# Attention and MLP on one core: masks ahead of the first scores, thirty copies on other engines, a fourth buffer, and another order of all items

## The chip, the cores and the metric

One core of a Trainium2 chip runs the whole program. The metric is the device time of one execution in microseconds. The kernel before takes 229.18 us (median of three runs, 229.06 to 229.55).

## What is computed

Inputs q, k, v have 4 batches x 8 heads x 768 positions x 64, in float32. Heads 0, 2 and 6 see all earlier positions (they are called retrieval heads here); the other five see the first 4 positions and a window of 64 (stream heads). The heads' outputs, side by side, are the 3072 x 512 input of an MLP with a learned slope for negative values:

```python
scores = q @ k.T / sqrt(64)                      # per batch and head
keep   = causal                  for heads 0, 2, 6
keep   = causal & (pos < 4 | rel < 64)   for the others
a = softmax(where(keep, scores, -1e9));  x = a @ v      # then (4*768, 512)
h = x @ w_in                                     # w_in 512 x 2048
g = maximum(h, 0) + alpha * minimum(h, 0)
out = g @ w_out                                  # w_out 2048 x 512
```

## The kernel before

**Segments.** Work on attention goes in 16 segments n, four to a batch; a segment is a pair of heads (line 99: (2,6), (1,5), (0,4), (3,7)), so segments 0, 4, 8, 12 hold two retrieval heads. The MLP goes in eight blocks t of 512 or 256 tokens, two to a batch.

**Items.** Every step is an item with a name, and a list of 1076 names, `ORDER` (line 14), says in which order they are emitted (line 806). An engine runs its own instructions in that order and nothing reorders them, so `ORDER` fixes the order on TensorE (PE), ScalarE (ACT), VectorE (DVE), GpSimd (POOL), and the order in which SyncE (SP) and POOL issue DMAs. The names, with n the segment, hh the head of the pair, m a part:

- `Lq`, `Lk`, `Lv`: loads of float32 rows into one of four buffers each of qf, kf, vf (lines 203 to 246), issued by SP. For n < 8, q rows are read as 1536-byte pieces and k as pieces of 1536 (retrieval) or 512 bytes (stream); v always, and q and k from n = 8, as rows of 256 bytes. `wi0` to `wi7` and `wo0` to `wo3` load the weights with a cast to bf16 on the way, issued by POOL (lines 690 to 697).
- `Cq`, `Ck`, `Cv`: casts to bf16; the strings at line 296 name the engine of each segment. `Tq`, `Tk` (n < 8): transposes on PE (line 355) of q and of both heads of k, and `tq`, `tk` copy them out of PSUM. From n = 8 a DMA transposes (`Dq`, `Dk`, on SP).
- `S`: scores on PE; `s`: exp on ACT. In segments 0 to 3 a mask is added on PE by a second matmul with the identity, right behind each score (lines 457 to 463); from segment 4 on DVE multiplies the exps by 0/1 masks (`m`, lines 473 and 526), which POOL builds (`nr`, `ns`, lines 658 and 662). Scores of segments from 4 on, of two heads, are gathered and emitted as a burst: each uses half of PE's rows, and the two halves run side by side (line 417); where one half has little work they run one after the other over all rows.
- `A`, `a`: product with v, and division by the sum; `X`: transposition into xT (by DMA, or on PE with a copy `x`).
- `P`, `p`, `g`: first MLP product on PE, max(-h, 0) on ACT into a buffer `neg`, and the slope on DVE (lines 588 to 611). `O`, `o`: second product and copy out on ACT, from where POOL (t < 6) or SP stores it. `L`, `l`: the last 128 rows in three column cuts. `warm`: matmuls on a zero tile.

**Order around the change.** PSUM has eight banks, given out at build time by `take` in the order of emission. The first MLP products (`P0`, `P1`: blocks 0 and 1) begin when the four segments of batch 0 are done, near 27 us, and fill PE until about 55 us; the transposes of segments 4 to 7 (`Tq5`, `Tk4`, `Tk5`, `Tk7`, `Tq4`, `Tk6`, `Tq6`) are strewn among them, and the scores of segment 4 follow. SP issues the loads for these segments in the order q5, k4, k5, k7, k6, q4, q6, v7, v5, q7, k8, v6, v4. A buffer is loaded again when its cast has been done.

Of the kernel before, what the change touches and what calls it, by code (L numbers as in the profile page):

```python
# [14 lines left out]
busy zero La id warm0 kz3 Lq0.0 sz1 vz2 nms nmr so1 vz0 Lq0.1 Lk1 warm8 warm5 warm3 kz1 qz0 one Lq1 Lk0 Ck0.0 Cq0.0  # L15
Tq0.0 tq0.0 Tk0.0 qz kz0 kz2 idf warm2 Lk2 tk0.0 Ck1.0 Ck1.1 Cq0.1 Tk1 S0.0.1 s0.0.1 Tq0.1 S0.0.0 Cq1 warm7 Lv0 tk1.0
sz2 vz1 vz3 Tq1 Lq2 Ck0.1 S0.0.2 s0.0.0 tk1.1 Tk0.1 Ck2.1 tq1 S1.1.0 s0.0.2 Ck2.0 warm4 tq0.1 nz0 s1.1.0 Cq2 tk0.1 Cv0
Lk3 S0.1.0 kfz0 Lv1 vo ro0 Ck3.1 s0.1.0 Lq3 Ck3.0 wi1 wi0 Cq3 sz0 S1.0.0 so2 Al s1.0.0 so0 al S0.1.1 s0.1.1 Lv2 Tq2
Tk2 tk2.1 tk2.0 S0.1.2 S1.0.1 A0.0 s0.1.2 a0.0 Cv1 A0.1 a0.1 Cv2 s1.0.1 tq2 S1.1.1 nz1 Tk3 S2.0.1 tk3.0 s1.1.1 S2.0.2
X0 s2.0.1 x0 wi6 s2.0.2 wi7 Lv3 Lq5 Tq3 tk3.1 S2.0.0 wi5 m4.0.2 warm6 S2.1.0 A1.0 a1.0 Lk4 s2.0.0 A2.0 S2.1.1 A1.1  # L20
a2.0 tq3 s2.1.0 a1.1 S3.0.0 s2.1.1 s3.0.0 A2.1 a2.1 S3.1.1 X1 S3.0.1 s3.0.1 Lk5 wi4 kfz2 Cv3.0 Cq5 Lk7 wi2 X2 Ck4.0
s3.1.1 S3.1.0 x1 P0.0.0 x2 P0.0.1 A3.0 P0.1.0 P0.1.1 Lk6 Lq4 Lq6 Ck4.1 kfz3 nr Cv3.1 s3.1.0 A3.1 Lv7 Lv5 Lq7 Ck5.0 wi3
a3.0 P0.2.0 Tq5 tq5 P0.3.0 P0.3.1 a3.1 X3 x3 ns kfz1 P0.2.1 Tk4 near2 P1.2 P0.1.2 P0.2.2 P0.0.2 p1.2 p0.1 g0.1 Ck5.1
P1.0 P0.3.2 g1.2 P0.15 tk4.0 p0.2 g0.2 p0.15 wo0 p1.0 Lk8 near0 g0.15 g1.0 ro1 P1.12 P1.14 m12.1.2 p0.0 g0.0 wo1 tk4.1
p1.12 P0.14 g1.12 p0.14 g0.14 P0.13 p0.13 g0.13 P0.11 p1.14 Tk5 Ck7.1 g1.14 P1.10 tk5.0 p0.11 p1.10 Ck6.0 Ck7.0 g0.11
m8.0.2 tk5.1 wo2 Lv6 Lv4 P0.10 P0.8 p0.8 Tk7 g1.10 wo3 Cq4 Lk9 P0.12 P1.8 p0.10 g0.8 p0.12 g0.10 Tq4 P0.6 P0.9 p0.3
Ck6.1 g0.3 tq4 P0.4.0 P0.5.0 Tk6 P0.4.1 p1.8 g1.8 tk7.0 p0.9 g0.9 Cq6 P0.5.1 P0.5.2 p0.5 g0.12 p0.6 tk6.1 P0.4.2 g0.6
g0.5 tk6.0 S4.0.5 P0.7 p0.7 P1.6 g0.7 P1.4 s4.0.5 p0.4 Tq6 m4.1.2 tk7.1 g0.4 Cv5 p1.6 g1.6 O0.1.0 tq6 S4.0.3 O0.2.0
O0.2.1 S5.1.1 S5.0.0 S4.0.1 S6.1.0 m14.0.2 p1.4 g1.4 s5.0.0 O0.1.1 s4.0.3 s4.0.1 O0.2.2 S5.0.2 S5.1.0 S4.0.2 S5.1.2
s6.1.0 m4.0.1 Cv7 O0.3.0 s5.0.2 s5.1.2 s5.1.1 s4.0.2 O0.1.2 s5.1.0 O0.1.3 o0.1 Cq7 Cv4 O0.3.1 m5.1.0 m8.1.2 m5.0.2  # L30
m4.0.3 m5.1.2 S4.0.0 S4.1.4 S5.0.1 S4.0.4 S4.1.0 s4.0.4 s5.0.1 Lk10 m5.0.1 O0.2.3 O0.3.2 Tq7 m5.0.0 o0.2 s4.1.0 m4.0.4
m5.1.1 A5.1 s4.0.0 m4.0.0 a5.1 O0.3.3 tq7 S7.0.0 S7.0.1 S4.1.3 S7.1.1 S6.0.5 S4.1.1 m4.0.5 s4.1.4 o0.3 Lq9 s4.1.3 Ck8
m4.1.3 A5.0 a5.0 X5 s4.1.1 A4.0 s7.0.0 s7.1.1 Lk11 Lq8 s7.0.1 a4.0 s6.0.5 near1 m7.0.0 m7.1.1 m4.1.0 O1.1.0 S7.1.0
S6.0.4 S7.0.2 S4.1.5 S6.0.1 S7.1.2 S6.1.1 O1.1.1 Cv6 s7.1.0 O1.0.0 s4.1.5 m7.0.1 s6.1.1 m4.1.5 m6.1.1 s7.1.2 m6.1.0
s7.0.2 m7.0.2 S6.0.2 S4.1.2 S6.1.2 S6.0.0 s6.0.4 s4.1.2 s6.0.1 s6.1.2 O1.0.1 m6.0.5 m7.1.0 m4.1.1 m4.1.4 m7.1.2 m6.1.2
S6.0.3 A4.1 s6.0.0 m6.0.0 m6.0.1 A7.1 O1.1.2 A6.1 s6.0.3 m6.0.4 m6.0.3 s6.0.2 a4.1 a6.1 A6.0 A7.0 a6.0 O1.1.3 O0.0.0
O0.0.1 O0.0.2 O1.0.2 m10.0.2 O1.0.3 O0.0.3 o0.0 X4 X6 a7.1 a7.0 X7 P2.9 P2.3 p2.9 P3.4 Ck9 Cq9 g2.9 P2.14 p2.14 g2.14
Cq8 p3.4 Lq10 Lq11 Dk8.0 P2.10 p2.10 Dk9.1 o1.0 p2.3 g2.3 g3.4 Dk8.1 P3.2 P3.14 P3.12 P2.8 Dq8 P2.1 P3.8 o1.1 p3.2
Dk9.0 Lv10 g2.10 Dq9 p3.14 P2.7 Ck10 g3.2 p3.12 g3.12 g3.14 P2.2 p2.2 g2.2 Cq10 Dq10 P2.11 p2.1 g2.1 p2.11 p2.8 g2.11
P3.6 P2.5 p2.5 g2.5 P2.13 p2.13 g2.8 g2.13 P2.0 p2.0 g2.0 p2.7 P3.0 p3.0 P2.4 S8.0.5 Lv8 Lv11 P2.15 P2.12 s8.0.5 Cq11  # L40
g3.0 p2.15 g2.7 g2.15 S8.0.0 p2.12 g2.12 Ck11 p3.6 S9.0.2 P2.6 p2.6 g3.6 s8.0.0 p2.4 g2.4 g2.6 s9.0.2 p3.8 P3.10 g3.8
p3.10 O3.0.0 O2.0.0 S8.1.5 s8.1.5 O3.0.1 O2.0.1 g3.10 m8.0.0 Cv8 S8.1.3 S9.0.0 S8.0.3 S9.1.1 S8.0.1 S9.1.0 s8.1.3
s9.1.0 s8.0.1 s9.0.0 s8.0.3 m8.0.3 m8.0.1 O2.0.2 O2.0.3 o2.0 Dk10.1 Lv9 m9.0.0 Cv9 m8.0.5 Dk11.0 m9.1.0 m9.0.2 S8.0.4
S9.0.1 S10.1.1 S8.1.4 Dq11 s8.1.4 Lq13 Lk13 O3.0.2 Dk10.0 s9.1.1 s10.1.1 s9.0.1 s8.0.4 O3.0.3 o3.0 Dk11.1 S10.1.0
S10.1.2 m9.0.1 S11.0.2 S9.1.2 S8.0.2 S11.0.0 s9.1.2 Cv10 m9.1.1 A9.0 s11.0.2 s10.1.0 O2.3.0 m9.1.2 A9.1 a9.0 a9.1 X9
s10.1.2 s11.0.0 O2.3.1 Lq15 Lv14 Lq12 S8.1.0 S11.0.1 S10.0.3 m10.1.0 s8.0.2 S10.0.1 S8.1.2 S8.1.1 S10.0.0 O2.3.2
s8.1.2 s8.1.0 m8.1.4 Cq13 s11.0.1 s8.1.1 m11.0.2 m10.1.2 m8.0.4 m11.0.0 A8.0 s10.0.0 m8.1.5 m10.1.1 O2.3.3 a8.0
S11.1.2 S10.0.4 S11.1.0 S10.0.5 S10.0.2 m8.1.3 m11.0.1 s10.0.3 s10.0.1 S11.1.1 s11.1.2 A10.1 s11.1.1 O2.2.0 O2.1.0
s10.0.4 m6.0.2 m10.0.1 Cv11 m8.1.1 m8.1.0 a10.1 m10.0.4 Ck13 m10.0.0 m11.1.2 A11.0 A8.1 O2.1.1 s10.0.2 s10.0.5 o2.3
s11.1.0 Dk13.0 m11.1.1 m10.0.3 m10.0.5 m11.1.0 A10.0 a11.0 a8.1 a10.0 O3.1.0 A11.1 Cq12 O2.2.1 O2.2.2 O2.2.3 a11.1 X8  # L50
# [796 lines left out]
```

## Time and profile before

| | |
|---|---|
| median of three runs | 229.18 us (229.06 to 229.55) |
| the profiled execution | 229.83 us, its span 228.0 us |
| matmuls on PE | 2005 |
| last matmul ends / span ends | 225.0 / 228.0 us |
| DMA over the span | 37.39 MB, mean 164 GB/s |

Busy time by stretch of the span, in us:

| stretch | PE | DVE | ACT | POOL | DMA share | GB/s |
|---|---|---|---|---|---|---|
| 0 to 30: batch 0's attention | 28.1 | 23.5 | 18.9 | 23.9 | 1.04 | 244 |
| 30 to 54: MLP blocks 0 and 1, first product | 24.0 | 18.1 | 21.4 | 8.2 | 1.19 | 222 |
| 54 to 78: batch 1's attention, second product | 23.3 | 18.0 | 18.5 | 3.6 | 0.97 | 207 |
| 78 to 103: blocks 2 and 3, first product | 25.0 | 16.9 | 13.2 | 1.6 | 0.99 | 192 |
| 103 to 126: batch 2's attention | 23.0 | 20.6 | 17.7 | 3.2 | 1.05 | 192 |
| 126 to 150: blocks 4 and 5, first product | 24.0 | 14.3 | 12.2 | 1.7 | 1.11 | 212 |
| 150 to 183: batch 3's attention | 33.0 | 22.5 | 19.9 | 3.1 | 0.51 | 102 |
| 183 to 205: blocks 6 and 7, first product | 22.0 | 13.7 | 12.0 | 0.5 | 0.06 | 25 |
| 205 to 228: their second product | 20.1 | 4.1 | 5.8 | 0.0 | 0.19 | 69 |

The DMA share is the mean busy share of the core's 16 DMA engines; it can pass 1 because transfers on one engine overlap. In the page and the views that follow, a row gives start and length of a group of instructions, the engine, the line, output <- inputs, and in brackets how long the engine stood idle before it and what ended that.

### The profile page before, as it was taken

How to read it: one execution, taken by the hardware profiler on the slowest of the kernel's cores; microseconds unless marked ns; L12 is line 12 of the kernel's file. 1: busy time of each engine (PE TensorE's matmuls, PEld its weight loads, DVE VectorE, ACT ScalarE, POOL GpSimd, SP SyncE). 2: the span in 40 equal slices, each digit the busy share in tenths (PEclk: the TensorE clock that was granted, in tenths of full speed). 3: DMA queues.
4: the chain of work that ended last, by engine and by line, in shares of the span. 5: the costliest groups of instructions: out<-in, count | busy, mean ns of one | idle time of the engine just before them, and what ended most of it. 6: DMA issues, size and time to landing. Idle time of an engine off the chain costs nothing.

```text
span 228.0 us, 5239 instructions
## 1 busy us (share of the span) xinstructions
PE 222.4 (98%) x2005; PEld 135.9 (60%) x2005; DVE 151.6 (66%) x395; ACT 139.6 (61%) x284; POOL 45.8 (20%) x91
## 2 busy tenths in 40 slices
PE   8999999999999999999999999999999999999994
PEld 8789876563455656555556455556556555664454
DVE  7769849966389816899699219987586535966000
ACT  2689559999799128477994136787594236563311
POOL 6769996101130001000400001000110110000000
PEclk9999999999999999999999999999999999999999
DMA  6999999999998798989969899995821420000213
GB/s 190 313 229 210 286 223 262 206 197 241 206 287 142 132 204 227 172 192 181 254 153 199 194 266 146 218 166 107 132 93 38 116 95 0 0 4 0 88 66 123
DMA packets 95417, 37.39 MB, mean 164 GB/s; under 512 B 82440, under 2 KB 93600, under 8 KB 95392
## 3 DMA queue, kind: packets, MB, share of 16 engines
q1 hardware_dynamic: 89136, 27.73, 61.2%
q0 software_dynamic: 5792, 8.93, 17.1%
q10 hardware_dynamic: 464, 0.40, 0.5%
q8 instruction: 15, 0.25, 0.5%
q14 instruction: 10, 0.08, 0.2%
HBM read 27.71 MB, written 6.29 MB: 149 GB/s over the span
## 4 chain that ended last, share of the span: by engine, by line
PE 92%; ACT 3%; DVE 2%; issue 1%; DVEq 0%; ACTq 0%
PE P L597 35%; PE P L617 34%; PE P L552 7%; PE P L430 4%; PE P L687 3%; PE P L413 2%; PE P L363 2%; PE P L636 2%; ACT neg L602 1%; PE P L501 1%; DVE kT L392 1%; PE P L423 1%; PE P L577 1%; ACT kT L392 1%; ACT eS L523 1%
## 5 line engine op out<-in xcount | busy, mean ns | idle before, releaser
L609 DVE SCALAR_TENSOR_TENSOR g<-neg,oma,P 128x256 bf16<-128x256 f32 (+1 forms) x128 | 71.0, 608 | 35.9 <-ACT neg L602 35.5
L597 PE MATMUL P<-xT,w_in_b 128*128 128x512 bf16 (+1 forms) x512 | 86.5, 326 | 0.0
L617 PE MATMUL P<-w_out_b,g 128*128 128x512 bf16 x368 | 85.4, 379 | 0.0
L602 ACT ACTIVATE neg<-P 128x512 f32<-128x512 f32 x96 | 54.4, 600 | 27.2 <-PE P L597 22.6
L597 PEld LDWEIGHTS <-w_in_b 128*128 128x128 bf16 x512 | 49.5, 98 | 31.7 <-DVE g L609 0.2
L617 PEld LDWEIGHTS <-g 128*128 128x128 bf16 x368 | 33.8, 98 | 37.2 <-issue 1.2
L469 ACT ACTIVATE eR<-P 128x448 bf16<-128x448 f32 (+4 forms) x63 | 37.1, 636 | 5.4 <-PE P L430 2.3
L623 ACT COPY ot<-P 128x512 f32<-128x512 f32 x23 | 13.8, 602 | 37.8 <-PE P L617 32.9
L627 POOL DMA_DIRECT2D out_dram<-ot x18 | 10.3, 571 | 113.2 <-ACT ot L623 113.0
L517 ACT ACTIVATE eS<-P 128x352 bf16<-128x352 f32 x45 | 21.0, 493 | 3.7 <-PE P L430 3.7
L563 DVE TENSOR_TENSOR xn<-P,rcp 128x448 bf16<-128x448 f32 (+1 forms) x32 | 19.5, 608 | 1.1
L528 DVE TENSOR_TENSOR eS<-eS,ms_near 128x352 bf16<-128x352 bf16 x45 | 14.3, 334 | 4.4 <-ACT eS L517 4.2
L479 DVE TENSOR_TENSOR eR<-eR,mr_near 128x128 bf16<-128x128 bf16 (+5 forms) x54 | 12.1, 252 | 4.0 <-ACT eR L469 4.0
L430 PE MATMUL P<-qT,kT 64*128 64x176 bf16 (+13 forms) x181 | 11.7, 251 | 0.3 <-DVE g L609 0.3
L430 PEld LDWEIGHTS <-kT 64*128 64x128 bf16 x181 | 7.2, 94 | 7.6 <-issue 6.8
L413 PE MATMUL P<-qT,kT 128*128 128x192 bf16 (+14 forms) x68 | 11.3, 251 | 0.3 <-ACT eS L523 0.3
L552 PE MATMUL P<-vb,eS 128*128 128x65 bf16 x260 | 11.0, 193 | 0.4 <-DVE eS L528 0.4
L552 PEld LDWEIGHTS <-eS 128*128 128x128 bf16 x260 | 9.7, 97 | 2.9 <-DVE eS L528 0.6
L562 DVE RECIPROCAL rcp<-P 128x7 f32<-128x7 f32 (+1 forms) x32 | 6.3, 198 | 7.1 <-PE P L552 6.9
L552 PE MATMUL P<-vb,eR 128*128 128x65 bf16 x276 | 10.1, 192 | 0.0
L552 PEld LDWEIGHTS <-eR 128*128 128x128 bf16 x276 | 9.4, 97 | 1.2
L645 DVE COPY ot<-P 128x128 f32<-128x128 f32 x1 | 0.3, 292 | 14.3 <-PE P L636 14.3
(95 smaller groups left out, 175.5 us busy)
## 6 DMA issues: line engine op xcount, KB each, us to landing
out_dram<-ot POOLq DMA_DIRECT2D x18, 256.0 KB, 3.6
kf<-in_k_dram SPq DMA_DIRECT2D x21, 192.0 KB
qf<-in_q_dram SPq DMA_DIRECT2D x18, 192.0 KB
vf<-in_v_dram SPq DMA_DIRECT2D x14, 196.0 KB
qf<-in_q_dram SPq DMA_DIRECT2D x7, 384.0 KB
vf<-in_v_dram SPq DMA_DIRECT2D x12, 192.0 KB
w_in_b<-in_moe_w_in_dram POOLq DMA_DIRECT2D x8, 256.0 KB, 9.7
w_out_b<-in_moe_w_out_dram POOLq DMA_DIRECT2D x4, 512.0 KB, 13.4
```

Source lines behind the costliest of these rows:

```text
L413: nc.tensor.matmul(to, keys, queries, start=True, stop=stop)
L430: nc.tensor.matmul(to, keys[own], queries[own], start=True, stop=True)
L469: nc.scalar.activation(ebuf[n, hh][:, lo:hi].rearrange("p (x c) -> p x c", x=len(parts)), P[:, got[0]:got[0] + len(parts), 0:(hi - lo) // ...
L517: nc.scalar.activation(slots, sc[:, 0:352].rearrange("p (s c) -> p s c", c=176), AF.Exp, scale=scale)
L528: nc.vector.tensor_tensor(slots, slots, ms_near[:, 0:2, :] if m == 0 else ms_near[:, 1:3, :], op=ALU.mult)
L552: nc.tensor.matmul(pav[:, i, :], e[:, o:o + 128], vv[:, j, hh, 0:D + 1], start=(m == 0), stop=(m == len(terms) - 1))
L563: nc.vector.tensor_tensor(xn[n][:, 0:nt, D * hh:D * hh + D], pav[:, :, 0:D], rcp.to_broadcast([128, nt, D]), op=ALU.mult)
L597: nc.tensor.matmul(psg[:, w * i:w * (i + 1)], w_in_b[:, c, 128 * fb:128 * (fb + 1)], xT[:, c, o:o + w], start=(x == 0), stop=(x == 3))
L602: nc.scalar.activation(neg[t, f], bank(held["P", t, f][0]), AF.Relu, scale=-1.0)
L609: nc.vector.scalar_tensor_tensor(g_buf[t % 2][:, fb, 0:w], neg[t, f][:, c], oma[:, fb:fb + 1], bank(got[0])[:, c], op0=ALU.mult, op1=ALU.add)
L617: nc.tensor.matmul(bank(held["O", t, s][0]), g_buf[t % 2][:, f, 128 * s:128 * (s + 1)], w_out_b[:, f, :], start=(f == 0), stop=(f == 15))
L623: nc.scalar.copy(ot, bank(got[0]))
```

## The change

`ORDER` is new as a whole; the loads of k and v for segments 0 to 7 are two items each, one per head. A dictionary `ENGINE` names another engine for 30 items. `relu` has four `neg` buffers instead of three. For segment 0, head 0, two groups of mask matmuls become items `Z` of their own: they open the accumulation in PSUM, and the scores are added behind them (columns without a mask are written alone). The loads stay on their engines: `ENGINE` has no entry for a load.

```diff
 ORDER = """
...
-X0 s2.0.1 x0 wi6 s2.0.2 wi7 Lv3 Lq5 Tq3 tk3.1 S2.0.0 wi5 m4.0.2 warm6 S2.1.0 A1.0 a1.0 Lk4 s2.0.0 A2.0 S2.1.1 A1.1
-a2.0 tq3 s2.1.0 a1.1 S3.0.0 s2.1.1 s3.0.0 A2.1 a2.1 S3.1.1 X1 S3.0.1 s3.0.1 Lk5 wi4 kfz2 Cv3.0 Cq5 Lk7 wi2 X2 Ck4.0
-s3.1.1 S3.1.0 x1 P0.0.0 x2 P0.0.1 A3.0 P0.1.0 P0.1.1 Lk6 Lq4 Lq6 Ck4.1 kfz3 nr Cv3.1 s3.1.0 A3.1 Lv7 Lv5 Lq7 Ck5.0 wi3
-a3.0 P0.2.0 Tq5 tq5 P0.3.0 P0.3.1 a3.1 X3 x3 ns kfz1 P0.2.1 Tk4 near2 P1.2 P0.1.2 P0.2.2 P0.0.2 p1.2 p0.1 g0.1 Ck5.1
...
+tk2.0 A0.0 vz3 S0.1.2 Lk3.1 tk2.1 Lv1.0 Lv1.1 Lq3 Cq2 Tq2 Lv2.0 warm8 Lv2.1 tq2 wi0 Lv3.0 Lv3.1 Lq5 a0.0 s0.1.1 S1.0.1
+Ck3.1 s0.1.2 A0.1 Ck3.0 kfz0 Lk4.0 S1.1.1 s1.0.1 Cv1 ro0 Lv4.0 S2.0.1 s1.1.1 Tk3 s2.0.1 a0.1 S2.0.2 tk3.1 so1 A1.0
+a1.0 s2.0.2 S2.0.0 s2.0.0 Cq3 X0 wi6 x0 tk3.0 Tq3 tq3 Cv2 Lv5.1 wi7 wi5 kfz1 wi4 wi2 S2.1.1 A1.1 a1.1 S2.1.0 s2.1.1
+A2.0 m4.1.2 S3.1.1 s2.1.0 Lk4.1 kfz3 a2.0 Lk5.0 s3.1.1 S3.0.0 A2.1 s3.0.0 S3.0.1 a2.1 X1 Lv6.0 S3.1.0 s3.0.1 X2 x1
+P0.0.0 s3.1.0 Cv3.0 x2 A3.0 Cv3.1 P0.2.0 Lk5.1 Lk7.0 Ck4.0 a3.0 A3.1 a3.1 Lq7 P0.1.0 Cq5 P0.3.0 wi3 wo0 P0.0.1 nz1
+Lv6.1 Lk7.1 Lk6.0 P0.1.1 wo1 X3 Tq5 P0.2.1 Ck4.1 Tk4 P0.3.1 x3 P0.3.2 wo2 wo3 Lk6.1 Lq4 Lq6 Lv7.0 P0.2.2 p0.2 g0.2
...
+one Lk8 P0.12 g1.12 g1.2 p1.14 Lq9 g1.14 P0.14 p0.15 g0.15 p0.14 g0.14 P1.10 P0.10 p0.10 g0.10 p0.12 P0.11 p0.11 g0.11
+Ck5.0 Tk5 Ck7.0 Ck7.1 P0.8 P1.8 tk5.0 tk5.1 P0.5.0 p1.8 P0.5.1 tk4.1 P1.4 g0.12 p0.8 g1.8 p1.4 g1.4 Cq4 Tq4 S5.1.2
+s5.1.2 P0.5.2 p0.5 g0.8 Lk9 Cq6 tq4 P0.9 P0.13 p1.10 P0.4.0 P0.4.1 P0.4.2 g0.5 S4.0.1 near1 s4.0.1 Lv7.1 Lv4.1 p0.4
+g1.10 Ck6.0 P0.6 p0.6 P0.7 Lv5.0 near2 Cv6 p0.7 S4.1.4 Cv4 Tk7 g0.4 Lq8 Lv8 S4.1.0 s4.1.0 ns s4.1.4 g0.6 m8.0.2 O0.3.0
+Ck6.1 g0.7 tk7.0 nr Tq6 p0.13 O0.3.1 tq6 Cq7 tk7.1 S4.0.0 g0.13 p0.9 O0.2.0 g0.9 P1.6 Lv10 Tk6 tk6.1 tk6.0 S5.1.0
...
 """.split()
+
+ENGINE = dict(x.split(":") for x in """
+kz3:V Ck0.0:V Cq0.0:A kz0:P tk0.0:A Ck1.0:V Cq0.1:A Cq1:V so2:P tq2:V Ck4.1:A Cv3.1:P tk4.1:V Ck7.0:A tk7.0:V Cq6:P
+Cv7:P Cv6:P Ck10:P Cq11:P Ck11:P Cv8:P Cv10:A o2.1:V Ck12:P Cq14:P Cv14:P Cq15:P Ck15:A o5.1:V
+""".split())
...
+    def load_eng(name):
+        return {"S": nc.sync, "A": nc.scalar}[ENGINE.get(name, "A" if name == "Lk0.0" else "S")]
...
+    def masks_first(n, hh, m):
+        sc = score_bank(n, hh, m)
+        RM, RO, RB = tiles(n).RM, tiles(n).RO, tiles(n).RB
+        for x, part in enumerate(r_parts(n, m)):
+            lo, hi = RB[part], RB[part + 1]
+            first = True
+            for j in range(6):
+                a, y = max(lo, RO[j]), min(hi, RO[j] + RM[j])
+                if a < y:
+                    nc.tensor.matmul(sc[:, x, a - lo:y - lo], ident, nmr[:, causal(n, j), a - RO[j]:y - RO[j]],
+                                     start=first, stop=False)
+                    first = False
...
-        neg[t, f] = work.tile([128, 512], fp32, tag="neg", name="neg", bufs=3)
+        neg[t, f] = work.tile([128, 512], fp32, tag="neg", name="neg", bufs=4)
...
+        for name, load, to in (("Lq", load_q, 1), ("Lk", load_k, 8), ("Lv", load_v, 8)):
+            if n < to:
+                for hh in range(2):
+                    item(f"{name}{n}.{hh}", load, n, [hh])
```

SP's loads behind q5, as the new order issues them: k4.0, v4.0, v5.1, k4.1, k5.0, v6.0, k5.1, k7.0, q7, v6.1, k7.1, k6.0, k6.1, q4, q6, v7.0, k8, q9, k9, v7.1, v4.1, v5.0, q8 (the figure behind the point is the head of the pair). On ACT the cast `Ck4.1` now stands between the last exp of segment 3 and the first `relu` of the MLP; it was on POOL. On POOL the masks `ns` and `nr` now stand behind the cast `Cv4`; they were ahead of the w_out loads.

## The prediction

> **What bounds the kernel now.** I read the page first, then what TensorE waited for, then the DMA queues in single stretches, then GpSimd's timeline, then the chain of waits.
>
> ```profile
> PE 222.4 (98%) x2005; PEld 135.9 (60%) x2005; DVE 151.6 (66%) x395; ACT 139.6 (61%) x284; POOL 45.8 (20%) x91
> DMA  6999999999998798989969899995821420000213
> ```
>
> PE is busy 98% of the span, so the sum of its matmuls is nearly the time. But the DMA line stands at 8 to 9 tenths from the first microseconds to about 155 us: until then anything that PE needs from DRAM is in a queue behind other transfers.
>
> ```profile
> PE P L687 <- DVE zero L288: 1.1, 1, 1.1
> PE P L363 <- DVE kT L394: 0.5, 1, 0.5
> PE P L552 <- DVE eS L528: 0.4, 1, 0.4
> PE P L413 <- ACT eS L523: 0.3, 2, 0.2
> PE P L430 <- DVE g L609: 0.3, 1, 0.3
> ```
>
> After its start PE waited 1.5 us by these rows, and no row names a load. That is a property of the order, not of spare DMA. The two queues that carry loads, q1 (SP: q, k, v) and q0 (POOL: the two weight matrices), from 42 to 51 us:
>
> ```profile
> q0 software_dynamic: 1413, 1.40, 91.4%
> q1 hardware_dynamic: 1413, 0.37, 30.2%
> ```
>
> The packet counts are equal; from 27 to 36 us they are 1260 and 1260. So two full queues take turns packet by packet, whatever a packet holds. SP's packets are then v rows of 256 bytes, POOL's hold 1 KB: SP gets 41 GB/s. From 57 to 63 us, with q0 empty, q1 moves 4927 packets in 6 us. A v head is 768 or 784 such rows: 0.95 us alone, 5.0 us beside weights (1413 in 9 us). Which cast waited for it:
>
> ```profile
> 40.58 0.83 POOL L315 CAST natq<-qf 128x768 bf16<-128x768 f32 x1 [2.77 <-DMA qf<-in_q_dram]
> ...
> 56.37 0.93 POOL L348 CAST vb<-vf 128x896 bf16<-128x896 f32 x1 [14.97 <-DMA vf<-in_v_dram]
> ```
>
> The first is Cq4: q of segment 4 arrives at 40.58 us. The second is Cv5: v5 arrives at 56.37. In SP's order everything up to v5 is q5, k4, k5, k7, k6, q4, q6, v7, v5, and by then all twelve weight loads are in too. The use on PE, from the chain of waits:
>
> ```profile
> 30.88 0.34 PE P L363 x6
> ...
> 44.18 0.34 PE P L363 x6
> ```
>
> These are Tk4 and Tq4, the transposes of k4 and q4 on PE.
>
> **The change, part by part.**
>
> *Loads.* In SP's list of the changed kernel the loads move against each other. After q5 stand: k4.0, **v4.0, v5.1**, k4.1, k5.0, **v6.0**, k5.1, k7.0, q7, **v6.1**, k7.1, k6.0, k6.1, **q4**, q6. Four v heads and q7 are now ahead of q4, and two v heads are ahead of k4's second head. POOL still issues the last six w_in loads and all four w_out loads between about 20 and 35 us (its casts before them have the old lengths), so q0 is full from about 23 to 50 us, as it was from 27 to 54.
>
> When does k4.1 land? Counting off the trace's packets by their size, SP had finished v3 at 24.4 us; so it will again (one w_in load is issued near 4 us instead of 16, so the same bytes have passed). Then q5 and k4.0, 384 rows of 1536 bytes or 24 per DMA engine, in pairs with weight packets at 0.17 us a pair (my estimate: from 27 to 36 us a pair took 9 us x 16 / 1260 = 0.114 with mostly 512-byte rows, and a row of 1536 bytes is longer): 4.1 us. Then v4.0 and v5.1: 2 x 5.0 = 10. Then k4.1, 8 pairs: 1.4. Sum 40.0, and about 0.6 until a cast sees it. The cast Ck4.1 now stands on ACT, behind the last exp of segment 3 and ahead of p0.2; 0.5 us for it (510 ns on POOL, the natm rows), so **Tk4 starts near 41 us**, not 30.9. PE has only P0.2.1 left in front of it and is in order, so it stands still for about 10 us; ACT too, with every relu behind the cast.
>
> When does q4 land? This needs no rule of sharing. Ahead of q4, itself included, are q5, q7, q4, k4 to k7, four v heads and all weights. Before, q5, q4, q6, k4 to k7, four v heads and all weights were in at 56.37. The same bytes in the same packets, q7 for q6, and the DMA engines are busy throughout in both. So q4 arrives at about 56.4. Cq4 takes 0.83, so **Tq4 starts near 57.3 us instead of 44.18: 13.1 us later**. Between Tk4 and Tq4 PE has 13.3 us of work in both kernels; Tk5 stands in between (k5.1 needs 24 + 48 + 24 more pairs, about 10.6 us after k4.1, then two casts of 0.5: near 52), so PE would stand ready for Tq4 at about 55.6. So q4 decides, and both earlier waits lie inside its 13.1 us.
> Bounds: from below 54.3 for Tq4, if one w_out load is still behind q4 (512 packets, each 9 us x 16 x 91.4% / 1413 = 0.093 us on one engine, so 3.0 us); from above 59, if DMA gaps in the first 6 us or a late POOL push it.
>
> *Everything before Tk4*: mask matmuls ahead of the scores (two groups, for segment 0 head 0), a dozen moved copies and memsets, warm-up matmuls in other places. By the rows PE's first useful 25 us could end 0.6 us sooner or 1 us later. Either way PE then waits for k4: the value is 0, hidden by the 10 us wait; without that cover it is -0.6 to +1.0.
>
> *PE's work.* I counted both PE lists with the trace's start-to-start time of each shape (216 ns for 512 columns, 109 for 256, 29 for 65, 56 for 128). Fifteen paired score bursts in place of seventeen, so more scores run over full height: 0.7 us more, less 2 x 0.2 us that a burst loses at its two ends: +0.3. It lies ahead of Tq4, where q4 covers it; behind Tq4 both lists hold 178.9 us.
>
> *Behind Tq4.* Before, PE took 225.0 - 44.2 = 180.8 us for these 178.9, so 1.9 us of waits. In the changed order GpSimd builds the masks of segments 4 and on behind Cv4, and v4.1 stands nine 256-byte heads and q6 behind q4: 9 x 0.95 + 1.1 = 9.7 us, so it lands at 66; Cv4 0.93, the stream masks 3.4 (30.81 to 34.25 in the timeline), the causal one 1.27: 71.7. DVE's first product with a mask, m4.1.4, waits for it with g1.6 and the products of segment 5 behind it, about 5.9 us, so A5.1 can start at 77.6; PE reaches it at 57.3 + 20.0 = 77.3. ACT has some 20 us of exps, relus and copies in the same 20. So this is tight: I take 0.5 us more than before, between -1 (the old waits vanish) and +3 (both engines late).
>
> *Eleven later casts to GpSimd, others between ACT and DVE*: DVE loses a dozen of 0.35 to 0.6 us and takes four copies, over 100 us in which PE names DVE for 0.4 and 0.3 us: value 0, bounds -0.7 and +1 (POOL's output DMAs stand behind casts that wait for loads, with three output buffers). *Fourth neg buffer*: ACT waited 3.3 us for DVE's products, but PE waited for neither: 0, at best -0.3. *End*: the last piece goes out by ACT instead of DVE and SP, 0.27 us against 0.29: 0, +-0.2.
>
> One rule of the Trainium skill I weigh against this. At the start 44 matmuls of the warm-up took 4.88 us, the next 14 took 0.89 us in the chain of waits, so for 5 us PE ran at half speed. "TensorE: Matmul & The Clock Gate", Part 1, says that the array returns to half clock after an idle window of about 3.4 us. By that rule the 10 us stop at Tk4 costs 2.5 us again: PE would stand ready for Tq4 at 56.9 instead of 55.6, still ahead of q4; the sum stays, only its lower end for Tq4 would rise to 56.9. No wait in this trace is long enough to show it.
>
> **Sum.** Tq4 57.3 + 178.9 + waits 2.4 = 238.6; + 3.0 from PE's last matmul to the span's end, as before (225.0 to 228.0) = span 241.6. The profiled execution took 229.83 for a span of 228.0, so 243.4; the median of the runs, 229.18, is 0.65 lower: **242.8 us**. With the bounds: 54.3 and 0.9 of waits give 238.3, 59 and 5 give 247.1.
>
> **Rivals.**
> - *The loads do not bind* and the kernel is **faster**. If v4, v5 and v6 slipped through without holding up q4, the cast of q4 would be done when PE gets there, at about 43.7; that is the point from which it decides: q4 in SBUF by 42.8. Then the startup gains 0.6, PE's waits of 0.3 and 0.4 us for DVE may go, +0.3 of work: 229.2 - 1.0 = 228.2. For it: before has no PE wait for a load. Against it: 1413 packets to 1413. Chance 0.07, and 0.03 that such gains and losses cancel within 0.2%.
> - *Partly held up.* The weights come later than I think, because POOL stands in front of a cast that waits, and SP has the DMA engines for itself meanwhile. If all four w_out loads (12 us of packets) fell behind q4, Tq4 would start at 45.3 and the time be 230.8; between one and four, 231 to 238. Against it: the casts ahead of the w_out loads need q5 and k4.0, which land by 29. Chance 0.11.
> - *More than held up.* ACT, blocked until 41, and DVE, waiting for masks until 72, stay behind PE in the dense stage that follows, where ACT was busy 18.5 of 24 us (54 to 78): 3 to 6 us on top, 247 to 251. Chance 0.09.
> - *My sum*, 238 to 247: 0.70.
>
> About 0.2% is what measurements of this kernel can tell from no change (229.06 to 229.55 in three runs). Slower 0.90, same 0.03, faster 0.07. The range of 234 to 248 leaves out the first rival and the far ends of the two others.
>
> **What would show it.** Right: in the changed profile Cq4 (POOL, natq<-qf) starts near 56 behind a DMA wait; six natm transposes near 41 stand behind ACT's cast of kf; q0 and q1 move equal packet counts from 27 to 45; a hole in PE's row between 30 and 41 and a second one before 57. Wrong: PE's row without holes there, or Tq4 before 53. If the holes are there but the time is over 247, the dense stage behind is at fault; if half-speed matmuls (107 ns for 128 columns) follow the hole, the clock rule holds.

## The result, and the profile after

The changed kernel takes 246.67 us, median of four executions (245.27 to 248.46); the kernel before took 229.37 beside it (229.06 to 229.89). The ratio is 1.0756, interval 1.068 to 1.0833. Ratios here and below are of undisturbed executions and medians of all, so a ratio is not always the quotient of two medians. The profiled execution is the slowest of the four: 248.46 us, span 246.8. PE's last matmul ends at 243.96 (before 225.09).

PE's row and the granted clock in 40 slices of 6.2 us:

```profile
PE   8896944993999999999999999899999999999995
PEclk9999796897699999999999999999999999999999
```

The holes are in the sixth and seventh slice (31 to 43 us) and in the tenth (from 56), with a smaller one in the fourth; the clock drops three times, in the slices from 25, 37 and 56 us. From 68 us on there is one small dent, at 154. What PE waited for (in all, times, longest):

```profile
PE P L377 <- ACT natm L344: 6.7, 1, 6.7
PE P L377 <- POOL natq L331: 3.7, 1, 3.7
PE P L592 <- POOL vb L362: 2.1, 1, 2.1
PE P L637 <- DVE g L649: 1.1, 1, 1.1
```

The first is Tk4, the second Tq4, the third A2.0 at 21.8 us, the last P4.11 at 154.6. Before, the longest wait after the start was 0.5 us. The two casts in front of the transposes, on ACT and on POOL:

```profile
39.84 0.51 ACT L344 CAST natm<-kf 128x384 bf16<-128x384 f32 x1 [9.68 <-DMA kf<-in_k_dram]
```

```profile
59.39 0.83 POOL L331 CAST natq<-qf 128x768 bf16<-128x768 f32 x1 [8.11 <-DMA qf<-in_q_dram]
...
68.64 0.94 POOL L362 CAST vb<-vf 128x896 bf16<-128x896 f32 x1 [5.72 <-DMA vf<-in_v_dram]
...
73.03 1.25 POOL L700 TENSOR_SCALAR_AFFINE_SELECT mr_near<-one 128x1248 bf16<-128x1248 bf16 x1
```

Each stood idle for a load. Tk4 starts at 40.41 and Tq4 at 60.27 (before 30.88 and 44.18 in the chain of waits, 30.71 and 44.02 in the timeline). The last two rows are Cv4 and the causal mask behind it, done at 74.3. The two load queues from 42 to 51 us (packets, MB, share of the DMA engines) again take turns:

```profile
q0 software_dynamic: 1251, 1.24, 81.2%
q1 hardware_dynamic: 1247, 0.75, 37.6%
```

Over the whole stretch from 27 to 45 us, for which the prediction had named equal counts as a sign, they are not equal:

```profile
q0 software_dynamic: 2337, 2.29, 83.9%
q1 hardware_dynamic: 3472, 1.33, 43.2%
```

Most of the difference lies between 34 and 39 us, where q0 moves 411 packets and q1 1378; POOL issues `wi3` and the w_out loads only from 32.9 to 37.4.

Where the 18.9 us by which PE ends later come from, I counted from PE's list: the time from each matmul to the next, less what its shape takes at full clock. The rest is standing still or half clock. Without it PE needs 217.4 us before and 217.7 after; the rest is 6.6 us before and 25.2 after. Of the 25.2: 7.4 until 30 us (before 4.5), 7.0 ahead of Tk4, 2.3 of half clock behind it, 3.9 ahead of Tq4, 2.6 of half clock behind it, 1.3 at 154.6, and 0.7 strewn over the rest.

### The profile page after: what moved, and what is told of

Read it like the earlier page. It is cut to its first block, busy times and chain, and to the rows that moved or that the text cites. A ratio compares the mean times of both kernels' runs of the same rounds, so it can differ in the third digit from the quotient of the medians.

```text
span 246.8 us, 5258 instructions
## 1 busy us (share of the span) xinstructions
PE 228.5 (93%) x2007; PEld 139.4 (56%) x2007; DVE 149.5 (61%) x386; ACT 138.9 (56%) x283; POOL 53.5 (22%) x101
## 4 chain that ended last, share of the span: by engine, by line
PE 72%; DMA 12%; SPq 8%; DVE 3%; issue 1%; ACT 1%; POOL 1%; ACTq 0%; DVEq 0%; POOLq 0%
PE P L657 30%; PE P L637 29%; DMA kf<-in_k_dram 5%; PE P L592 5%; PE P L444 4%; DMA vf<-in_v_dram 3%; DMA qf<-in_q_dram 3%; SPq L223 3%; DVE g L649 2%; SPq L238 2%; DMA kT<-natk 2%; PE P L437 1%; PE P L676 1%; SPq L262 1%; PE P L377 1%
## 5 line engine op out<-in xcount | busy, mean ns | idle before, releaser
L637 PE MATMUL P<-xT,w_in_b 128*128 128x256 bf16 (+1 forms) x512 | 91.0, 336 | 1.1 <-DVE g L649 1.1
L637 PEld LDWEIGHTS <-w_in_b 128*128 128x128 bf16 x512 | 51.0, 101 | 36.4 <-issue 5.7
L642 ACT ACTIVATE neg<-P 128x512 f32<-128x512 f32 x96 | 53.7, 601 | 23.3 <-PE P L637 21.5
L509 ACT ACTIVATE eR<-P 128x448 bf16<-128x448 f32 (+4 forms) x63 | 36.2, 626 | 6.4 <-PE P L437 2.8
L663 ACT COPY ot<-P 128x512 f32<-128x512 f32 x21 | 12.2, 588 | 43.4 <-PE P L657 42.6
L557 ACT ACTIVATE eS<-P 128x352 bf16<-128x352 f32 x45 | 20.1, 482 | 9.2 <-PE P L444 4.8
L362 POOL CAST vb<-vf 128x896 bf16<-128x896 f32 (+1 forms) x11 | 9.6, 869 | 34.6 <-PE P L444 24.7
L427 PE MATMUL P<-qT,kT 128*128 128x192 bf16 (+19 forms) x62 | 11.3, 262 | 0.0
L444 PE MATMUL P<-qT,kT 64*128 64x176 bf16 (+11 forms) x163 | 10.2, 250 | 0.0
L444 PEld LDWEIGHTS <-kT 64*128 64x128 bf16 x163 | 6.1, 94 | 6.4 <-issue 5.9
```

The source lines that it names most:

```text
L444: nc.tensor.matmul(to, keys[own], queries[own], start=True, stop=True)
L509: nc.scalar.activation(ebuf[n, hh][:, lo:hi].rearrange("p (x c) -> p x c", x=len(parts)), P[:, got[0]:got[0] + len(parts), 0:(hi - lo) // ...
L557: nc.scalar.activation(slots, sc[:, 0:352].rearrange("p (s c) -> p s c", c=176), AF.Exp, scale=scale)
L637: nc.tensor.matmul(psg[:, w * i:w * (i + 1)], w_in_b[:, c, 128 * fb:128 * (fb + 1)], xT[:, c, o:o + w], start=(x == 0), stop=(x == 3))
L642: nc.scalar.activation(neg[t, f], bank(held["P", t, f][0]), AF.Relu, scale=-1.0)
L663: cast_of("A", f"o{t}.{s}")(ot, bank(got[0]))
```

## Experiments

| run | us, median (range) | ratio to before | its interval |
|---|---|---|---|
| changed kernel | 246.67 (245.27 to 248.46) | 1.0756 | 1.068 to 1.0833 |
| kq_first | 248.79 (247.59 to 248.92) | 1.0832 | 1.0798 to 1.0865 |
| kqv_masks | 244.36 (240.26 to 246.58) | 1.0683 | 1.0611 to 1.0754 |
| before_new_loads | 236.82 (236.28 to 239.78) | 1.0348 | 1.0279 to 1.0417 |
| k4_first | 246.71 (245.43 to 247.61) | 1.0749 | 1.0702 to 1.0796 |
| weights_ahead | 245.38 (244.61 to 247.77) | 1.0697 | 1.0637 to 1.0756 |
| weights_held | 245.53 (244.35 to 247.87) | 1.0668 | 1.0617 to 1.072 |
| warm_fill | 250.08 (245.99 to 253.51) | 1.0785 | 1.0687 to 1.0884 |
| kqv_masks_start | 240.30 (239.24 to 240.85) | 1.0452 | 1.0416 to 1.0488 |
| old_front_new_rest | 244.01 (242.32 to 246.73) | 1.0623 | 1.0545 to 1.0701 |
| old_front_no_moved_casts | 244.87 (244.16 to 249.26) | 1.0659 | 1.0606 to 1.0711 |
| fourth_neg | 228.89 (228.10 to 229.56) | 0.9973 | 0.9946 to 1.0 |
| walls_removed | 238.56 (237.02 to 239.76) | 1.0392 | 1.0324 to 1.046 |

The kernels that wait for loads spread over 1.3 to 7.5 us from one execution to the next, the kernel before over 0.8 to 2.1 in its sets of runs. The diffs show the loads of SP in order, or one engine's items; what lies between is as it was.

### Is it the order of the loads? (before_new_loads, weights_ahead)

```diff
 SP, kernel before:
-q5 k4.0 k4.1 k5.0 k5.1 k7.0 k7.1 k6.0 k6.1 q4 q6 v7.0 v7.1 v5.0 v5.1 q7 v6.0 v6.1 v4.0 v4.1
+q5 k4.0 v4.0 v5.1 k4.1 k5.0 v6.0 k5.1 k7.0 q7 v6.1 k7.1 k6.0 k6.1 q4 q6 v7.0 v7.1 v4.1 v5.0
```

> The kernel before, with every item on its old engine and in its old place, a fourth neg buffer, and only the loads for segments 4 to 7 permuted over their 20 slots into the changed kernel's order (k and v one item per head). Theory: Ck4.1 near 40, Tk4 41 instead of 30.9; q4 lands near 56.5, Tq4 at 57 to 58 instead of 44.2; masks are early here, so the hole is all of it: 241 to 245 us. Rival (the loads alone do it only together with the moved casts): 229 to 233.

236.82: 7.3 us, less than half of the loss, and a miss. Tk4 waits 5.4 us, but the cast of q4 can start at 46.73 and Tq4 starts at 51.2 without a wait. As many bytes stand ahead of q4 on SP as in the changed kernel, so the other queue must differ. Its weights were late: POOL stood in Ck4.1, 7.97 us idle, with `wi3` and `wo0` to `wo3` behind it; they were issued at 37.8 and 42.4. The next run moves only those five.

```diff
 POOL:
-Ck4.1 kfz3 nr ... Ck5.0 wi3 ns ... Ck5.1 ... wo0 wo1 ... wo2 wo3
+wi3 wo0 wo1 wo2 wo3 Ck4.1 kfz3 nr ... Ck5.0 ns ... Ck5.1
```

> The run before_new_loads (before, with the changed order of loads) and only the last five weight loads moved: wi3 and wo0 to wo3 stand on POOL ahead of Ck4.1 instead of behind Ck4.1 and Ck5. In before_new_loads POOL stood 8 us in Ck4.1 waiting for k4.1 (35.55) and so issued these weights at 37.8 and 42.4; meanwhile SP had the DMA engines for itself, q4 landed at 44.8 and Tq4 never waited: 236.82 us. Theory (the forecast's q4 step needs POOL free to issue its weights; in the changed kernel Ck4.1 on ACT does that): with the weights issued near 28, q4 lands at 54 to 57, Tk4 at 40, Tq4 near 57 to 58, 241 to 245 us. Rival (POOL's casts, not its weight loads, make the difference): it stays at 236 to 238.

245.38, within 1.3 us of the changed kernel and 0.4 above the range: the kernel before, with nothing moved but loads (and the fourth neg buffer). Tk4 starts at 36.0, not 40; the cast of q4 starts at 56.5 and Tq4 at 59.6. The two queues from 33 to 41 us, first without, then with the five loads ahead:

```profile
q1 hardware_dynamic: 3756, 1.84, 111.5%
q0 software_dynamic: 116, 0.10, 7.8%
```

```profile
q0 software_dynamic: 1217, 1.20, 87.9%
q1 hardware_dynamic: 1218, 0.45, 32.8%
```

With POOL standing, SP moves 1.84 MB in these 8 us; with the weights issued, 0.45 MB. That is the cause of the late q4: v heads ahead of it **and** a weight queue that nothing holds back. Either one alone is not enough: before_new_loads has the v heads ahead, kq_first below has the free weight queue, and their Tq4 starts at 51.2 and 46.3. In before_new_loads a cast that waited on POOL was a gate for the weights. PE's worst wait here is not at Tk4 or Tq4 but at Tk7 (its cast on DVE waits 7.75 us for k7):

```profile
PE P L374 <- POOL natm L341: 6.6, 2, 5.7
PE P L374 <- DVE natm L341: 6.5, 1, 6.5
```

### Does q4 decide, or each hole by itself? (k4_first)

```diff
-k4.0 v4.0 v5.1 k4.1 k5.0
+k4.0 k4.1 v4.0 v5.1 k5.0
```

> The changed kernel with k4.1 ahead of v4.0 and v5.1 in SP's list, nothing else. Theory (q4 alone decides, and the stop at Tk4 lies inside it): the hole of 6.7 us ahead of Tk4 goes, but q4 lands where it did, so the stop ahead of Tq4 grows from 3.9 to about 12 us and the time stays: 245 to 248.5. Rival (each hole costs its length): 246.67 - 6.7 = 240.

246.71: no change, as the theory has it. The stop did not all move to Tq4, as I had written: 9.7 us of it stand ahead of Tk5, which starts at 52.96, and 0.6 ahead of Tq4, at 59.49:

```profile
PE P L377 <- POOL natm L344: 9.7, 1, 9.7
```

### What stands behind the holes? (kq_first, kqv_masks)

```diff
-q5 k4.0 v4.0 v5.1 k4.1 k5.0 v6.0 k5.1 k7.0 q7 v6.1 k7.1 k6.0 k6.1 q4 q6
+q5 k4.0 k4.1 k5.0 k5.1 q4 k7.0 k7.1 q6 k6.0 k6.1 q7 v4.0 v6.0 v6.1 v5.1
```

> The changed kernel with k and q ahead of the v heads in SP's list, in the same slots: q5, k4.0, k4.1, k5.0, k5.1, q4, k7.0, k7.1, q6, k6.0, k6.1, q7, v4.0, v6.0, v6.1, v5.1; everything else is kept. Theory (the order of the loads moved the end, by way of Tk4 and Tq4): Ck4.1 before 33.5 us, q4 in by about 40, no hole ahead of Tk4 and Tq4, so PE would reach A5.1 some 15.5 us sooner than the changed kernel's 83.0 (13.2 of stop and 2.4 of half clock behind Tq4), at 67.4. But v4.1 and the masks behind Cv4 are where they were: as many bytes are ahead of v4.1, so Cv4 again waits until about 67 and the masks are done near 73 to 74. By the theory the next thing late is therefore the masks: A5.1 at 79 to 80, a new hole ahead of it, time 242 to 247. Rival (holes are the whole loss and what lies behind has slack): 229.5 to 232. Second rival (the loss comes from casts and masks on other engines, and the holes are a symptom): Tk4 and Tq4 stay late.

248.79, 1.8 above the theory's range. Tk4 starts at 32.6 and Tq4 at 46.3, both without a hole. Then PE stands 14.3 us from 61 to 75.3, because DVE stands for the mask, which POOL builds behind Cv4:

```profile
DVE eR L519 <- POOL mr_near L700: 15.9, 1, 15.9
```

```profile
PE P L444 <- DVE g L649: 14.3, 1, 14.3
```

So the loss has a second wall of the same height: the first O0.2.3 behind it starts at 76.4 here, and at 78.1 in the changed kernel, where PE came late enough not to notice. Mending the two holes is worth nothing while the masks stand behind Cv4.

```diff
-q5 k4.0 v4.0 v5.1 ... k6.1 q4 q6 v7.0 k8 q9 k9 v7.1 v4.1 v5.0
+q5 k4.0 k4.1 k5.0 k5.1 q4 k7.0 k7.1 q6 k6.0 k6.1 v6.0 v6.1 v4.0 v4.1 q7 v5.0 v5.1 v7.0 v7.1 k8 q9 k9
 POOL:
-wo2 wo3 ... Cv6 Cv4 ns Ck6.1 nr
+wo2 wo3 ns nr ... Cv6 Cv4 Ck6.1
```

> As the run before it, and besides v6, v4, q7, v5, v7 in this order behind k6 and ahead of k8, q9, k9, and the masks ns and nr (with the memset they read) on POOL right behind the last w_out load instead of behind Cv4; ENGINE, buffers and all other items as changed. Theory: no hole at Tk4, Tq4 or A5.1; 246.67 - 15.6 = 231.0 us, 229.5 to 233. If moved casts and the rest of the order cost by themselves, it stays above 235.

244.36, profiled in its fastest execution (240.26): above the range, below the changed kernel by less than the runs scatter. The hole ahead of the masks is gone and others show:

```profile
PE P L437 <- ACT kT L408: 3.3, 1, 3.3
PE P L377 <- POOL g L331: 2.1, 1, 2.1
```

The first comes from q7, which my new list put behind v4: its cast on ACT waited for it until 59.44, and the copies of k6 out of PSUM stand behind that cast.

### Taking the walls away one by one (kqv_masks_start, old_front_new_rest, walls_removed)

```diff
 SP:   q7 from behind v4.1 to ahead of v6.0
 POOL: wi1 from near 4 us to beside wi0
 ACT:  Ck15 from ahead of p5.2 to behind p4.7
```

> The run kqv_masks with three more items moved: q7 ahead of v6 in SP's list (there its cast stood on ACT until 60.3 with the copy of k6 behind it: a stop of 3.5 us and 2.7 us of half clock), wi1 beside wi0 instead of near 4 us (v2 landed at 21.3 instead of 18.3 in the changed kernel; a stop of 2.2 us near 20), and Ck15 behind g4.7 (1.3 us at 146). Theory: these stops go, sum 3.5 + 2.7 + 2.2 + 1.3 = 9.7 less 0.5 for what is late next: kqv_masks profiled at a span of 238.3, so span 229 and 229 to 232 us. Rival (wi1 does not set v2, the startup stays late): 231.5 to 234.

240.30: a miss. Two of the three stops went (q7, Ck15), the one of A2.0 did not (3.3 us at 22), and behind them stood a new one, 5.0 us ahead of A5, with half clock after it. Its row on DVE:

```profile
DVE natk L350 <- DMA kf<-in_k_dram: 6.3, 1, 6.3
```

That is Ck9, a cast of the next batch's k. The new order has it on DVE among the mask products of segments 4 and 5, and k9's last packet comes at 67.5.

```diff
 DVE:
-g1.6 Ck9 m5.1.0 ... Cq8 ... Ck8 m5.1.1 ... m7.0.0 ...
+g1.6 m5.1.0 ... m5.1.1 ... m7.0.0 Ck9 Cq8 Ck8 ...
 POOL:
-wi1 wi0 ... Cq3 wi6 Cv2 wi7
+Cq3 Cv2 wi0 wi1 wi6 wi7
```

> The run kqv_masks_start with six more items moved: the casts Ck9, Cq8 and Ck8 from between and ahead of the mask products of segments 4 and 5 to behind those of 5 and most of 6 (ahead of the load Lq12), and wi0, wi1, wi6 on POOL from ahead of Cv2 to right behind it. In kqv_masks_start DVE stood 6.3 us in Ck9 until k9 was in (68.85), PE stood 1.1 and 3.9 us ahead of A5 and ran at half clock behind it; and v2 landed at 21.1, PE stood 3.3 us near 22 and the granted clock was 0.7 in the slice after it. Theory (in the new order each cast that waits for a load blocks what is queued behind it, and DMA lands everything late; PE's own work is the same): 5.0 + 2.7 + 3.3 + 1.8 = 12.8 less what is late next: 240.3 - 12.8 = 227.5 at best, 228 to 232. Rival (a part of the loss lies in the new order of the work itself, in PE's list or in the moved casts): 235 or more.

244.01: a miss, and mostly by my own edits. No stop is left between 33 and 80 us, but:

```profile
PE P L637 <- DMA w_in_b<-in_moe_w_in_dram: 6.8, 1, 6.8
PE P L637 <- DMA xT<-xn: 5.6, 3, 2.0
```

The first product waited for the weights that I had put late, and half clock followed. And the load of q12 on SP waited for Cq8, which I had put late too, with the DMAs behind it that transpose the attention output. One thing was settled: with wi0, wi1 and wi6 all behind Cv2, v2 is in at 17.9 and v3 at 21.4, against 21.3 and 27.0 in the changed kernel; moving wi1 alone had left v2 at 21.1.

```diff
 POOL:
-Cv1 Cq3 Cv2 wi0 wi1 wi6
+Cv1 wi0 wi1 Cq3 Cv2 wi6
 SP:
-Lq12 X5 Lk11 ... X4 X6 X7
+X5 ... X4 X6 X7 Lk11 Lq12
```

> The run old_front_new_rest with four moves that mend what my own edits there brought: wi0 and wi1 on POOL behind Cv1 instead of behind Cv2 (PE waited 6.8 us for them at 26 and ran at half clock behind it), and the loads Lk11 and Lq12 on SP behind X7 (Lq12 waited for Cq8, which I had moved later, so the DMAs that transpose the attention output into xT were late: 5.6 us at 89 to 96 and 2.2 us of half clock). Theory (no part of the loss lies in PE's work, in the moved casts or in the fourth buffer; it is a row of waits for loads, each standing behind the one before it): PE's own work is 218.8 us here and 218.4 in the kernel before; 244.0 - 6.8 - 2.0 - 5.6 - 2.2 = 227.4, plus what is late next: 227.5 to 233 us. Rival (another wait of the same kind fills what these leave, since too many bytes are due before 70 us in this order): 234 to 240. If it stays at 242 or more, these waits were not what decides and the cause is open.

238.56: the rival's range, not the theory's. What is left:

```profile
PE P L637 <- DMA xT<-xn: 4.8, 3, 2.0
PE P L637 <- DMA w_in_b<-in_moe_w_in_dram: 1.9, 1, 1.9
```

Counted as in the section on the result, PE's own work is 217.7 us in this run too, as in the changed kernel (the expectation counts it some 1 us higher, in both kernels alike); waits and half clock are 15.8 instead of 25.2. So no more than 0.3 us of the difference that these profiles show lies in PE's work. But I did not find a version of the new order that comes back to 229: each wait that went uncovered another one for a transfer. Whether the rest of the order could reach it was not settled.

### Holding the weights back in the changed kernel (weights_held)

```diff
 POOL (Ck4.1 was on ACT):
-Ck4.0 Cq5 wi3 wo0 nz1 wo1 wo2 wo3 ... Cv4 ns Ck6.1 nr
+Ck4.0 Cq5 nz1 Ck4.1 wi3 nr ns wo0 wo1 wo2 wo3 ... Cv4 Ck6.1
```

> The mirror of it on the changed kernel: Ck4.1 back on POOL, and wi3, the memset and the masks nr and ns, and wo0 to wo3 behind it; loads in the changed order, all other items as changed. Theory: POOL stands at Ck4.1, SP has the DMA engines, k4.1 in near 37.5 and Tk4 near 38.5, q4 in near 48, so PE reaches Tq4 at 54 without a stop and without half clock behind it, and the masks are long done: 246.67 - 6.3 - 2.4 = 238 us, 236 to 240.5. If the order of the loads alone set q4, as the forecast's sum said, Tq4 stays near 60 and the time at 245 to 248.

245.53: a miss. Tq4 did start 5.9 us sooner, at 54.35, but behind a stop of 3.9 us: the cast of q4 could start only at 53.5, and q4 had been expected near 48. The time is in the range that was written for the other case, Tq4 is not. In this order POOL stands in Cv2 until 24.5 us, so four w_in loads are issued only from 25.8 to 28.4 and share the DMA engines in the very time in which SP should have had them alone. Of the gain, 3.3 us went at 93.5 to 97.2 in waits for the transposes into xT, and half clock followed. That is consistent with the last series and not shown by an edit of its own.

### Is it the clock? (warm_fill)

```diff
-g1.4 Cq4 Tq4
+g1.4 Cq4 warm9 Tq4      (warm9: 60 more matmuls of 128 columns)
```

> The changed kernel with a warm-up item of 60 more matmuls of 128 columns right ahead of Tq4 (3.4 us of PE work at 56 ns each, in the 3.9 us in which PE stands there). Theory (the slow matmuls of 61 to 66 us, 430 ns for 512 columns instead of 216, are the clock after a stop): with the stop filled they take 216 ns, PE gets ahead by 2.4 us up to the masks, which are done at 74.3; the first product that waits for them was reached 2.4 us late, so the time falls by 1.5 to 2.6 us, to 244 to 245. Rival (the slow matmuls have another cause, such as DMA traffic): they stay at 430 ns and the time at 246 to 247.5.

The clock, yes: PE behind Tq4 in the changed kernel, then with the stop filled (start, length, count):

```profile
60.27 0.82 PE L377 MATMUL P<-ident,natq 128*128 128x128 bf16 x6 [3.71 <-POOL natq L331]
60.89 0.58 PE L437 MATMUL P<-qT,kT 128*128 128x176 bf16 x3
61.27 5.12 PE L637 MATMUL P<-xT,w_in_b 128*128 128x512 bf16 x13
```

```profile
57.83 3.51 PE L728 MATMUL P<-busy 128*128 128x128 bf16 x60
61.35 0.51 PE L377 MATMUL P<-ident,natq 128*128 128x128 bf16 x6
61.70 0.36 PE L437 MATMUL P<-qT,kT 128*128 128x176 bf16 x3
62.11 2.75 PE L637 MATMUL P<-xT,w_in_b 128*128 128x512 bf16 x12
```

Thirteen products take 5.12 us behind a stop, twelve take 2.75 behind the filler. The time did not fall, 250.08 with a spread of 7.5 us: in the profiled execution, the slowest of the four, all loads were later (k4.1 in at 40.9 instead of 39.3), and PE ran into the masks again (2.15 us at 76.1). What the half clock cost in the end is not settled by it.

### The small parts (fourth_neg, old_front_no_moved_casts)

```diff
 kernel before:
-        neg[t, f] = work.tile([128, 512], fp32, tag="neg", name="neg", bufs=3)
+        neg[t, f] = work.tile([128, 512], fp32, tag="neg", name="neg", bufs=4)
```

> The kernel before with a fourth neg buffer and nothing else (loads of k and v for segments 0 to 7 are named one per head, in the old order). The forecast gave this buffer 0, at best -0.3: 229.0 to 229.9 us. Rival (the buffer lets ACT run ahead, and DVE's or PE's waits shrink): under 228.7.

228.89 against 229.25, between the two ranges that I had written. The ratio is 0.9973, interval 0.9946 to 1.0: some 0.4 us faster perhaps, and no difference is just inside.

```diff
 in old_front_new_rest:
-ENGINE = dict(... thirty items ...)
+ENGINE = {}
```

> The run before it with every one of the thirty moved copies and casts back on its old engine (ENGINE empty), the order the same. Theory (moved copies and casts are worth nothing as long as their loads are in time): within 1.5 us of old_front_new_rest. Rival (eleven late casts on POOL cost by themselves): 2 us or more faster than it; (they are a gain): 2 us or more slower.

244.87 against 244.01, with intervals that overlap nearly whole: thirty moved copies and casts, worth nothing that these runs can tell, in an order that waits for loads. In an order that does not wait it wasn't tried.

## Why the prediction was right, and where not

- **Queues that take turns packet by packet; v heads ahead of k4 and q4.** Right where both queues are full: 1251 to 1247 packets from 42 to 51 us. That they are both full from 27 to 45 was wrong (2337 to 3472). before_new_loads and weights_ahead differ from the kernel before in loads alone (and in the fourth neg buffer, which fourth_neg prices at nothing or -0.4) and give +7.3 and +15.6 us.
- **Tk4 near 41.** 40.41; k4.1's last packet at 39.3 against a count of 40.0. This is luck, since two errors cancel: SP was done with v3 2.6 us later than counted (next item), and from there to k4.1 it took 12.3 us where the sum has 15.6. In that stretch the weight queue was not full all the time (from 34 to 39 us it moved 411 packets to SP's 1378).
- **Tq4 at 57.3, bounds 54.3 to 59.** 60.27, outside. The term that was too small is the start: I let SP finish v3 at 24.4 "again", since the same bytes have passed. It was 27.0; from there to the cast of q4 it took 32.4 us, and 32.0 in the kernel before from the end of v3 to the cast of v5, so the rest of this count held. wi0 and wi6 are issued ahead of Cv2 now, and v2, v3 share with them; moved behind it, v3 is in at 21.4. "Everything before Tk4" was bounded by +1.0 and was +3.0 (PE stands ready for Tk4 at 33.7; in before_new_loads, with the old start, at 30.7). It was hidden there as I said, but the same lateness reached q4, where nothing hides it.
- **"This needs no rule of sharing."** Wrong as a reason. The same bytes stand ahead of q4 in before_new_loads, and its cast starts at 46.7 there. It needs POOL to have issued the weights. In the changed kernel it had, by 37.4, since Ck4.1 is on ACT, so the number came out. I had this as a rival (POOL in front of a cast that waits, 231 to 238) and did not see that the kernel before, given this order of loads, works that way.
- **q4 decides, both earlier waits lie inside.** Right: k4_first took Tk4's hole away, and the time stayed.
- **PE's own work +0.3.** 217.7 against 217.4.
- **Behind Tq4: 2.4 us of waits.** 183.7 - 178.9 = 4.8, inside the bounds of 0.9 to 5. It is 2.6 of half clock, 1.3 at P4.11 and 0.9 of small ones. At P4.11 Ck15, now on ACT, waits 2.1 us for a buffer that a DMA still reads, with a relu behind it, and the g behind that is what PE waits for. The masks, which I called tight at 71.7, were done at 74.3 and cost nothing visible; kq_first shows that they were the next wall, some 2 us behind.
- **The clock rule.** By the rule of the Trainium skill, "TensorE: Matmul & The Clock Gate", Part 1, half clock follows an idle window. The trace agrees: behind Tk4 five products of 512 columns start 427 ns apart, where 216 is the time at full clock, and behind Tq4 thirteen take 5.12 us. "The sum stays" was wrong: I applied it to the first stop only. The second one, 1.7 us in my sum, was 3.7 and brought 2.6 us that nothing hides.
- **Casts to POOL, fourth buffer, tail: 0.** Nothing measurable, nothing measurable, and 2.8 us instead of 3.0. One of the casts that moved to ACT did cost something: Ck15 is the 1.3 us at P4.11, and kqv_masks_start, which has it behind p4.7, does not have that stop.

The sum for the span was 241.6, the profiled span 246.8: +3.0 at Tq4, +2.4 behind it, -0.2 at the end. The profiled execution was the slowest, so the median is only 3.9 above the forecast. The mechanism was right: v heads ahead of q4, beside a full weight queue, and PE in front of Tq4. That the time fell inside the range owes something to luck: the profiled execution, at 248.46, lies above the 247.1 that the bounds of the sum give.

Two small readings of the prediction are off and change nothing: the DMA row has a few digits of 6 and 7 before 155 us, and the terms for k4.1 add up to 39.9.

## What to carry to other kernels

Before a load is moved, write down who issues into the other queues at that time and what holds that issuer back: a cast that waits for its load, on the engine that issues the weights, is a gate, and moving that cast to another engine opens it. Behind a removed wait look for the next one: here k4, q4, the masks, k9 and the transposes into xT stood one behind the other, and no step of the series bought more than the 5.5 us from old_front_new_rest to walls_removed. And where PE stands for about 2 us or more, count the half clock behind the stop as well, unless a later wait covers it.

## What was not expected of the hardware

A stop far shorter than those at Tk4 and Tq4 can already bring half clock. In the changed kernel PE stood 2.11 us from 21.8 on; PE's granted clock is the third number from the right in these rows (stretch, length, busy time of PE and of the others, clock, DMA share, GB/s):

```profile
22.00:24.00 2.00, 0.06 (x3) 0.06 (x3) 0.78 (x3) 0.68 (x1) 0.98 (x2) 1.00 1.29 173
24.00:26.00 2.00, 2.00 (x37) 1.96 (x37) 0.83 (x2) 0.24 (x1) 2.00 (x5) 0.66 1.26 196
26.00:28.00 2.00, 2.00 (x23) 1.93 (x22) 0.27 (x2) 1.06 (x2) 1.88 (x5) 0.50 1.14 306
```

In walls_removed a stop of 1.91 us at 26.3 left it at 1.00:

```profile
26.00:28.00 2.00, 0.26 (x5) 0.09 (x2) 0.56 (x1) 0.72 (x1) 0.80 (x3) 1.00 1.21 234
28.00:30.00 2.00, 1.83 (x31) 1.30 (x32) 0.78 (x2) 0.51 (x1) 2.00 (x4) 1.00 1.18 210
```

In k4_first one of 1.78 us did too, in kqv_masks one of 2.08 us did not (clock 0.50 from 24 to 26 us). The same page and part of the Trainium skill give the idle window as about 3.4 us and say that it runs free, without regard to the kernel. The 2.1 us stops here are shorter than that, and the measurement decides: the clock can fall without a stop as long as the window.

Where the window begins makes the difference. In all fourteen profiles each change of the granted clock lies a whole number of times 3.41 us behind the first. In the windows of 3.41 us that this gives, the stop in the changed kernel lies whole in one (21.24 to 24.65), and so does the one in kqv_masks (19.41 to 22.82). The ones in walls_removed and k4_first are cut in two, at 27.08 and at 23.23. Taken over all windows at full clock, each of the 36 in which PE stood for 2.0 us or more in sum was followed by half clock. Of the 891 in which it stood for 1.63 us or less, one was, in the first 9 us of old_front_no_moved_casts. What lies between 1.63 and 2.0 us no profile shows.
